# Two orders at the start of a dense block: the third group's first products ahead of the first second product, and the finished rows' norm two calls later

## The chip, the cores and the metric

The kernel runs on one core of a Trainium2 chip. The metric is device time in microseconds (us) of one execution, the median of several runs. The engines are TensorE (PE; its weight loads are PEld), VectorE (DVE), ScalarE (ACT), GpSimd (POOL) and SyncE (SP), which here only issues transfers (DMAs).

## The reference

Four layers are applied in turn to x, 2048 rows by 576, in 32-bit floats: attention, dense, attention, dense, each on a layer norm of x and added back to x. The attention layer is linear attention with 32 heads of 18, on softmax feature maps. The dense layer has 4608 hidden features:

```python
def _A_ref(x, wqkv, w_phi, wo):
    q, k, v = ...                                  # x @ wqkv, 32 heads of 18
    pq, pk = q @ w_phi, k @ w_phi                  # per head
    phi_q = concat(softmax(pq), softmax(-pq)); phi_k = concat(softmax(pk), softmax(-pk))
    kv = sum_s phi_k v;  z = sum_s phi_k
    o = (phi_q kv) / (phi_q z + 1e-6)
    return o @ wo
def _B_ref(x, w1, b1, w2, b2):
    r = relu(x @ w1 + b1)
    return (r * r) @ w2 + b2
x = x + _A_ref(layernorm(x)); x = x + _B_ref(layernorm(x))
x = x + _A_ref(layernorm(x)); x = x + _B_ref(layernorm(x))
```

## The kernel before

The rows are worked in four blocks of 512. One pair of attention and dense is called a layer here (0 and 1). Before each layer's dense blocks a barrier finishes the sums over all keys. Then come four dense blocks, in the order 3, 2, 0, 1 for layer 0 and 1, 0, 3, 2 for layer 1. Names such as m_0acc leave the layer's number out: m_0 is the dense work of block 0, n_0 the norm of block 0's finished rows, a_0 the attention of block 0.

Products are made of high and low halves: a 32-bit operand is split into a rounded high part (a copy on ACT) and the remainder (a subtraction on DVE, for one piece on POOL), and three of the four partial products are summed.

A dense block (`g_mlp`) takes the hidden features in 36 groups of 128. For one group f:

- `first(f)` loads w1's and w2's pieces by SP (lines 666 and 169 for w1, 668 for w2), copies their high halves on ACT (L673 for w1, L674 for w2) and subtracts the low halves (L676 and L677 on DVE, L678 on POOL). It also takes the PSUM tile for the group's hidden values.
- `hidden(f)` is the first product, 14 matmuls (L688): five with the high weights and high rows, four with the low rows, five with the low weights. Groups 0 and 1 are done in two halves of 256 columns, since the last rows of the block arrive late.
- `square(f)` makes the relu (L695), the high square (L696) and the square again (L697) on ACT and the low half on DVE (L698).
- `second(f)` is the second product into five PSUM accumulators: 12 matmuls by rows (L715) and 3 by features (L706). The high squares are read first, the low ones by the last four L715 and the last L706.

The steady step f is first(f + 1), hidden(f), square(f), second(f - 1). After group 35 comes the tail: the last second product, and the adding of the accumulators to the rows x (L755, L759), which are stored and kept for the next block's use.

All this is written as a generator with a yield behind each step, 36 yields in a block. `weave` draws on a second generator, `g_back`, beside it: at rate 1.0 one call for each step, at rate 1.5 (layer 0, blocks 2 to 4 in order) 54 calls in 36 steps, and what is left is drained behind the tail. In layer 0 `g_back` first norms the rows of the block finished just before (`g_norm`, 5 calls: statistics on DVE, L298 and L299; two steps on POOL, L300 and L301; scaling on DVE, L303 and L304; then transposes on PE, L318 and L328, whose results ACT and DVE write in two halves, L319, L320, L330 and L331). Then it makes that block's values (4 calls) and keys (10 calls) for the next layer. Then, in both layers, it makes the attention of the block that comes next (34 calls): queries (L359, L378), softmax, sums, output projections (L642, L645) and the next block's norm. The last call of that is the norm's last turn.

The text's order is not each engine's order. A planner takes, on each engine, the earliest instruction in the text among those that it expects to be ready, by its own durations; the order is fixed when the program is built, and each engine then waits on semaphores. Tiles are taken from rings: two buffers each for the w1 and w2 pieces raw and split, and for the squared values; two PSUM buffers "w" for projections, transposes and group 1's hidden values; one PSUM buffer "h" for the hidden values of all other groups; five buffers for rows x.

Of the kernel before, what the change touches and what calls it, by code (L numbers as in the profile page):

```python
# [13 lines left out]
P = 128  # L14
# [7 lines left out]
def layers_kernel(  # L22
# [632 lines left out]
    def g_mlp(layer, b, x, after, name, behind=None):  # L655

        xh, xl = x["h"], x["l"]
        acc = [ps_a.tile([P, TB], F32, tag=f"acc{c}", name=f"{name}acc{c}") for c in range(NC)]
        parts = {}
        R = D - P  # L660

        def first(f, behind=None):
            cols = slice(f * P, (f + 1) * P)
# [4 lines left out]
            nc.sync.dma_start(r2, w2[cols])  # L668
# [4 lines left out]
            nc.scalar.activation(h1, r1, AF.Copy)  # L673
            nc.scalar.activation(s2[:, :D], r2, AF.Copy)  # L674
            with tc.issue_after(behind.ins) if behind else nullcontext():
                nc.vector.tensor_sub(l1, r1, h1.bitcast(F32))  # L676
                nc.vector.tensor_sub(s2[:, D : D + R], r2[:, :R], s2[:, :R].bitcast(F32))  # L677
            nc.gpsimd.tensor_sub(s2[:, D + R : 2 * D], r2[:, R:], s2[:, R:D].bitcast(F32))  # L678
            ph = wtile(f"{name}ph{f}") if f == 1 else ps_a.tile([P, TB], F32, tag="h", name=f"{name}ph{f}")
            parts[f] = (h1, l1, s2, ph)  # L680

        def hidden(f, cols):
            h1, l1, s2, ph = parts[f]
            ops = [(h1[:, c], xh[:, c, cols]) for c in range(NC)]
            ops += [(h1[:, c], xl[:, c, cols]) for c in range(KC)]
            ops += [(l1[:, c], xh[:, c, cols]) for c in range(NC)]
            for k, (a, m) in enumerate(ops):
                nc.tensor.matmul(ph[:, cols], a, m, start=(k == 0), stop=(k == len(ops) - 1))  # L688

        def square(f):  # L690
            s2, ph = parts[f][2:]
# [3 lines left out]
            nc.scalar.activation(hr, ph, AF.Relu, bias=b1t[:, f : f + 1])  # L695
            nc.scalar.activation(hh, hr, AF.Square)  # L696
            nc.scalar.activation(hr, hr, AF.Square)  # L697
            dense["last"] = nc.vector.tensor_sub(hl, hr, hh.bitcast(F32))  # L698
            parts[f] = (s2, hh, hl)

        def features(f, ks):
            s2, hh, hl = parts[f]
            hi, lo = s2[:, R:D], s2[:, D + R : 2 * D]
            for k in ks:
                a, m = ((hi, hh), (lo, hh), (hi, hl))[k]
                nc.tensor.matmul(acc[KC], a, m, start=(f == 0 and k == 0), stop=(f == NF - 1 and k == 2))  # L706

        def by_rows(f, ts, ks):
            s2, hh, hl = parts[f]
            hi, lo = s2[:, :R], s2[:, D : D + R]  # L710
            for t in ts:
                rows = slice(t * P, (t + 1) * P)
                for k in ks:
                    a, m = ((hh, hi), (hh, lo), (hl, hi))[k]
                    nc.tensor.matmul(acc[t][:, :R], a[:, rows], m, start=(f == 0 and k == 0),  # L715
                                     stop=(f == NF - 1 and k == 2))

        def second(f):

            for ks in ((0, 1), (2,)):  # L720
                by_rows(f, range(NT), ks)
                features(f, ks)
            del parts[f]

        every = slice(0, TB)
        halves = (slice(0, TB // 2), slice(TB // 2, TB))
# [3 lines left out]
        for f in range(2):  # L730
            hidden(f, halves[1])
            square(f)
        second(0)
        yield
        yield
        first(2)
        for f in range(2, NF):
            if f + 1 < NF:
                first(f + 1)
            hidden(f, every)  # L740
            square(f)
            second(f - 1)
            yield
# [100 lines left out]
    for layer in range(2):  # L844
# [4 lines left out]
        for i, b in enumerate(order):  # L849
# [64 lines left out]
```

## Time and profile before

| | |
|---|---|
| median of 3 runs | 2573.97 us (2573.57 to 2576.54) |
| profiled execution, span | 2573.9 us |
| PE busy | 2529.2 us |
| DVE, ACT, POOL busy | 1455.2, 1235.7, 623.0 us |
| HBM traffic | 246.90 MB read, 30.97 MB written |

The profile is of one execution. Its span reaches from the first to the last instruction, and it agrees with the median; no other time of that execution is listed. A row of the order of time has the start, the busy time, the engine, the line, the operation, what is written from what, the sizes and the count; brackets give the idle time before it and what ended it. Matmuls are pipelined, so a row's busy time overlaps the next row's, and the time from start to start is what a matmul costs in a stream.

### The profile page before, as it was taken

To read this page: it belongs to the slowest core of one execution; us is meant where nothing else is said; L and a number is where in the kernel's file an instruction comes from. 1 tells how busy PE (TensorE), PEld (TensorE's weight loads), DVE (VectorE), ACT (ScalarE), POOL (GpSimd) and SP (SyncE) were. 2 spreads that over 40 slices of the span, in tenths; PEclk is the share of its full clock that TensorE was granted. 3 is DMA by queue.
4 is the path that set the end of the run, shared out by engine and by line. 5 is a ranking of instruction groups with operands and counts; after the bars stand their busy time and mean duration, and the time that the engine had idled before them with its cause. 6 is when DMAs were issued, how large, how long until landed. Compare 5 with 4: busy or idle time off the path is not lost.

```text
span 2573.9 us, 41327 instructions
## 1 busy us (share of the span) xinstructions
PE 2529.2 (98%) x15456; PEld 2231.5 (87%) x15456; DVE 1455.2 (57%) x2254; ACT 1235.7 (48%) x2061; POOL 623.0 (24%) x693
## 2 busy tenths in 40 slices
PE   8999999999999999999999999999999999999999
PEld 7998888888888888888888988888888888888887
DVE  7778844456665467556434778444564458444333
ACT  4344554445554455545544445545555455534444
POOL 3543311113222132223111333121231213121111
PEclk9998999999999999999999999999999999999999
DMA  8212333354333543343334123335433353334332
GB/s 251 75 27 67 104 111 87 110 187 129 91 93 113 171 126 97 87 140 101 108 98 122 43 67 103 111 94 161 130 101 88 101 167 103 87 102 130 98 101 79
DMA packets 298020, 280.61 MB, mean 109 GB/s; under 512 B 28186, under 2 KB 238362, under 8 KB 295770
## 3 DMA queue, kind: packets, MB, share of 16 engines
q1 hardware_dynamic: 296560, 275.26, 36.0%
q8 instruction: 121, 1.98, 0.3%
q10 hardware_dynamic: 1258, 2.70, 0.3%
q14 instruction: 81, 0.66, 0.1%
HBM read 246.90 MB, written 30.97 MB: 108 GB/s over the span
## 4 chain that ended last, share of the span: by engine, by line
PE 55%; DVE 3%; POOL 1%; issue 1%; ACT 1%; DMA 0%; DVEq 0%; POOLq 0%; ACTq 0%; SPq 0%
PE m_1ph L688 8%; PE m_0ph L688 6%; PE m_1acc L715 6%; PE m_0acc L715 5%; PE m_2ph L688 5%; PE m_3ph L688 4%; PE m_3acc L715 3%; PE m_2acc L715 3%; PE m_1acc L706 2%; PE m_0acc L706 1%; PE m_2acc L706 1%; PE m_3acc L706 1%; PE a_2po L642 1%; PE t1opo L642 1%; PE k_0kp L359 1%
## 5 line engine op out<-in xcount | busy, mean ns | idle before, releaser
L715 PE MATMUL m_3acc<-m_3s,m_3hb 128*128 128x448 f32 x864 | 199.7, 366 | 1.0 <-DVE m_3hb L698 1.0
L715 PE MATMUL m_1acc<-m_1s,m_1hb 128*128 128x448 f32 x864 | 199.2, 366 | 1.5 <-DVE m_1hb L698 1.5
L715 PE MATMUL m_0acc<-m_0s,m_0hb 128*128 128x448 f32 x864 | 199.3, 366 | 1.3 <-DVE m_0hb L698 1.3
L715 PE MATMUL m_2acc<-m_2s,m_2hb 128*128 128x448 f32 x864 | 199.2, 366 | 1.3 <-DVE m_2hb L698 1.3
L688 PE MATMUL m_0ph<-a_0nh,m_0h 128*128 128x512 f32 (+1 forms) x760 | 192.7, 383 | 0.5 <-DVE m_0h L676 0.5
L688 PE MATMUL m_2ph<-a_2nh,m_2h 128*128 128x512 f32 (+1 forms) x760 | 191.9, 382 | 0.2 <-DVE m_2h L676 0.2
L715 PEld LDWEIGHTS m_0acc<-m_0s,m_0hb 128*128 128x128 f32 x864 | 161.7, 188 | 23.3 <-DVE m_0hb L698 2.2
L715 PEld LDWEIGHTS m_1acc<-m_1s,m_1hb 128*128 128x128 f32 x864 | 161.8, 188 | 23.0 <-DVE m_1hb L698 2.3
L715 PEld LDWEIGHTS m_2acc<-m_2s,m_2hb 128*128 128x128 f32 x864 | 161.8, 188 | 22.9 <-DVE m_2hb L698 2.2
L715 PEld LDWEIGHTS m_3acc<-m_3s,m_3hb 128*128 128x128 f32 x864 | 161.6, 188 | 22.8 <-DVE m_3hb L698 1.4
L676 DVE TENSOR_TENSOR m_2h<-m_2r,m_2h 128x640 fp32r<-128x640 f32 x72 | 62.9, 873 | 182.5 <-ACT m_2h L673 179.9
L688 PEld LDWEIGHTS m_0ph<-a_0nh,m_0h 128*128 128x128 f32 x760 | 136.5, 188 | 27.2 <-DVE m_0h L676 1.0
L688 PEld LDWEIGHTS m_2ph<-a_2nh,m_2h 128*128 128x128 f32 x760 | 136.8, 188 | 26.8 <-DVE m_2h L676 0.7
L676 DVE TENSOR_TENSOR m_3h<-m_3r,m_3h 128x640 fp32r<-128x640 f32 x72 | 66.4, 923 | 157.4 <-ACT m_3h L673 151.0
L676 DVE TENSOR_TENSOR m_0h<-m_0r,m_0h 128x640 fp32r<-128x640 f32 x72 | 65.6, 911 | 154.6 <-ACT m_0h L673 152.8
L676 DVE TENSOR_TENSOR m_1h<-m_1r,m_1h 128x640 fp32r<-128x640 f32 x72 | 64.9, 902 | 155.4 <-ACT m_1h L673 152.5
L678 POOL TENSOR_TENSOR m_2s<-m_2r,m_2s 128x128 fp32r<-128x128 f32 x72 | 61.2, 850 | 362.1 <-ACT m_2s L674 343.5
L678 POOL TENSOR_TENSOR m_0s<-m_0r,m_0s 128x128 fp32r<-128x128 f32 x72 | 58.8, 817 | 351.8 <-ACT m_0s L674 318.7
L678 POOL TENSOR_TENSOR m_3s<-m_3r,m_3s 128x128 fp32r<-128x128 f32 x72 | 59.2, 822 | 342.6 <-ACT m_3s L674 312.3
L695 ACT ACTIVATE m_3hr<-m_3ph,b1t 128x512 f32<-128x512 f32 x72 | 49.5, 687 | 186.6 <-PE m_3ph L688 181.7
L678 POOL TENSOR_TENSOR m_1s<-m_1r,m_1s 128x128 fp32r<-128x128 f32 x72 | 59.6, 828 | 322.0 <-ACT m_1s L674 312.5
L695 ACT ACTIVATE m_0hr<-m_0ph,b1t 128x512 f32<-128x512 f32 x72 | 49.4, 686 | 175.9 <-PE m_0ph L688 173.3
(1535 smaller groups left out, 6376.4 us busy)
## 6 DMA issues: line engine op xcount, KB each, us to landing
m_3r<-in_B_w SPq DMA_DIRECT2D x72, 288.0 KB
m_2r<-in_B_w SPq DMA_DIRECT2D x72, 288.0 KB
m_0r<-in_B_w SPq DMA_DIRECT2D x72, 288.0 KB
m_1r<-in_B_w SPq DMA_DIRECT2D x72, 288.0 KB
m_3r<-in_B_w SPq DMA_DIRECT2D x72, 256.0 KB
m_2r<-in_B_w SPq DMA_DIRECT2D x72, 256.0 KB
m_0r<-in_B_w SPq DMA_DIRECT2D x72, 256.0 KB
m_1r<-in_B_w SPq DMA_DIRECT2D x72, 256.0 KB
```

The costliest lines, as they stand in the source:

```text
L359: nc.tensor.matmul(pt[:, :HP], a, m, start=(k == 0), stop=(k == len(ops) - 1))
L642: nc.tensor.matmul(pt[:, :HP], a, m[:w, g], start=(g == 0 and k == 0), stop=(g == NG - 1 and k == 2))
L676: nc.vector.tensor_sub(l1, r1, h1.bitcast(F32))
L678: nc.gpsimd.tensor_sub(s2[:, D + R : 2 * D], r2[:, R:], s2[:, R:D].bitcast(F32))
L688: nc.tensor.matmul(ph[:, cols], a, m, start=(k == 0), stop=(k == len(ops) - 1))
L695: nc.scalar.activation(hr, ph, AF.Relu, bias=b1t[:, f : f + 1])
L706: nc.tensor.matmul(acc[KC], a, m, start=(f == 0 and k == 0), stop=(f == NF - 1 and k == 2))
L715: nc.tensor.matmul(acc[t][:, :R], a[:, rows], m, start=(f == 0 and k == 0), stop=(f == NF - 1 and k == 2))
```

## The change

`first` is cut in two: `first_one` (w1's piece, its split and the PSUM tile) and `first_two` (w2's piece and its split); `first` calls both. At the start of a dense block, `first_one(2)` and `hidden(2)` are written behind the squares of groups 0 and 1, ahead of the first two yields; `second(0)`, `first_two(2)`, `square(2)`, `first(3)` and `second(1)` stand behind those yields. The loop then runs from group 3. A block still has 36 yields. In `g_back` two bare yields stand ahead of the norm of the finished rows, so that this norm, and what follows it, comes two calls later in blocks 2 to 4 of layer 0.

```diff
+        def first_one(f, behind=None):
             cols = slice(f * P, (f + 1) * P)
             r1 = sb.tile([P, NC, P], F32, tag="r1", name=f"{name}r1_{f}")
-            r2 = sb.tile([P, D], F32, tag="r2", name=f"{name}r2_{f}")
             nc.sync.dma_start(r1[:, :KC], w1[: KC * P, cols].rearrange("(c p) n -> p c n", p=P))
             load_twice(r1[:, KC], w1, f * P, P)
...
+            nc.scalar.activation(h1, r1, AF.Copy)
+            with tc.issue_after(behind.ins) if behind else nullcontext():
+                nc.vector.tensor_sub(l1, r1, h1.bitcast(F32))
+            ph = wtile(f"{name}ph{f}") if f == 1 else ps_a.tile([P, TB], F32, tag="h", name=f"{name}ph{f}")
+            parts[f] = (h1, l1, ph)
+
+        def first_two(f, behind=None):
+            cols = slice(f * P, (f + 1) * P)
+            r2 = sb.tile([P, D], F32, tag="r2", name=f"{name}r2_{f}")
+            nc.sync.dma_start(r2, w2[cols])
             s2 = sb.tile([P, NC * HP], F32R, tag="s2", name=f"{name}s2_{f}")
-            nc.scalar.activation(h1, r1, AF.Copy)
             nc.scalar.activation(s2[:, :D], r2, AF.Copy)
...
         for f in range(2):
             hidden(f, halves[1])
             square(f)
-        second(0)
+        first_one(2)
+        hidden(2, every)
         yield
         yield
-        first(2)
-        for f in range(2, NF):
+        second(0)
+        first_two(2)
+        square(2)
+        first(3)
+        second(1)
+        yield
+        for f in range(3, NF):
             if f + 1 < NF:
                 first(f + 1)
             hidden(f, every)
...
                     xk = {}
+                    yield
+                    yield
                     yield from g_norm(lambda t: rows[t], xk, f"n{m}")
```

More of the change, by code (lines that the diff above doesn't have):

```diff
@@ L658, in g_mlp @@
         acc = [ps_a.tile([P, TB], F32, tag=f"acc{c}", name=f"{name}acc{c}") for c in range(NC)]
-        parts = {}
+        parts, wide = {}, {}
         R = D - P
         def first(f, behind=None):
+            first_one(f, behind)
+            first_two(f, behind)
+        def first_one(f, behind=None):
             cols = slice(f * P, (f + 1) * P)
             r1 = sb.tile([P, NC, P], F32, tag="r1", name=f"{name}r1_{f}")
-            r2 = sb.tile([P, D], F32, tag="r2", name=f"{name}r2_{f}")
             nc.sync.dma_start(r1[:, :KC], w1[: KC * P, cols].rearrange("(c p) n -> p c n", p=P))
             load_twice(r1[:, KC], w1, f * P, P)
-            nc.sync.dma_start(r2, w2[cols])
             hl1 = sb.tile([P, NC * HP], F32R, tag="h1", name=f"{name}h1_{f}")
@@ L671, in first @@
             l1 = hl1[:, NC * P : 2 * NC * P].rearrange("p (c n) -> p c n", n=P)
+            nc.scalar.activation(h1, r1, AF.Copy)
[7 more added lines that the diff above has]
+            nc.sync.dma_start(r2, w2[cols])
             s2 = sb.tile([P, NC * HP], F32R, tag="s2", name=f"{name}s2_{f}")
-            nc.scalar.activation(h1, r1, AF.Copy)
             nc.scalar.activation(s2[:, :D], r2, AF.Copy)
             with tc.issue_after(behind.ins) if behind else nullcontext():
-                nc.vector.tensor_sub(l1, r1, h1.bitcast(F32))
                 nc.vector.tensor_sub(s2[:, D : D + R], r2[:, :R], s2[:, :R].bitcast(F32))
             nc.gpsimd.tensor_sub(s2[:, D + R : 2 * D], r2[:, R:], s2[:, R:D].bitcast(F32))
-            ph = wtile(f"{name}ph{f}") if f == 1 else ps_a.tile([P, TB], F32, tag="h", name=f"{name}ph{f}")
-            parts[f] = (h1, l1, s2, ph)
+            wide[f] = s2
         def hidden(f, cols):
-            h1, l1, s2, ph = parts[f]
+            h1, l1, ph = parts[f]
             ops = [(h1[:, c], xh[:, c, cols]) for c in range(NC)]
@@ L698, in square @@
             dense["last"] = nc.vector.tensor_sub(hl, hr, hh.bitcast(F32))
-            parts[f] = (s2, hh, hl)
+            parts[f] = (hh, hl)
         def features(f, ks):
-            s2, hh, hl = parts[f]
+            s2, (hh, hl) = wide[f], parts[f]
             hi, lo = s2[:, R:D], s2[:, D + R : 2 * D]
@@ L708, in by_rows @@
         def by_rows(f, ts, ks):
-            s2, hh, hl = parts[f]
+            s2, (hh, hl) = wide[f], parts[f]
             hi, lo = s2[:, :R], s2[:, D : D + R]
@@ L722, in second @@
                 features(f, ks)
-            del parts[f]
+            del parts[f], wide[f]
         every = slice(0, TB)
```

2 lines of the change are left out of this document (1 added, 1 removed).

## The prediction

> **What bounds the kernel now.** I read the page first, then the waits of TensorE (PE), then the order of time at the start of a dense block, then at its end.
>
> ```profile
> span 2573.9 us, 41327 instructions
> PE 2529.2 (98%) x15456; PEld 2231.5 (87%) x15456; DVE 1455.2 (57%) x2254; ACT 1235.7 (48%) x2061; POOL 623.0 (24%) x693
> ```
>
> PE is the bound and nothing else is near it. The change issues the same matmuls in another order, so it can only move PE's idle time, which is 2573.9 - 2529.2 = 44.7 us over everything. A gain is small by nature; a loss has no such limit. PE's waits in the first 20 us of dense blocks 2, 3 and 4 of layer 0, in that order, are the ones that the change can reach (waiting instruction, releaser, us in total, times, longest):
>
> ```profile
> PE n_3p L318 <- DVE n_3n L303: 0.5, 1, 0.5
> PE m_2acc L715 <- DVE m_2hb L698: 0.5, 1, 0.5
> PE a_2np L318 <- DVE a_2nn L303: 0.4, 1, 0.4
> PE n_3p L328 <- DVE n_3l L320: 0.2, 1, 0.2
> ```
> ```profile
> PE n_2p L318 <- DVE n_2n L303: 0.5, 1, 0.5
> PE m_0acc L715 <- DVE m_0hb L698: 0.5, 1, 0.5
> PE n_2p L328 <- DVE n_2l L320: 0.4, 1, 0.4
> ```
> ```profile
> PE n_0p L328 <- DVE n_0l L320: 0.5, 1, 0.5
> PE n_0p L318 <- DVE n_0n L303: 0.5, 1, 0.5
> PE m_1acc L715 <- DVE m_1hb L698: 0.5, 1, 0.5
> ```
>
> The same three in each block: a transpose of the finished rows waits for their scaling (L318 on L303); the second product waits for the low half of the squared values (L715 on L698); a later transpose waits for a PSUM buffer to be emptied (L328 on L320). The order of time shows why, here in the third block (start us, us, engine, line, what, idle before):
>
> ```profile
> 837.38 0.69 ACT L695 ACTIVATE m_0hr<-m_0ph,b1t 128x512 f32<-128x512 f32 x1 [4.13 <-PE m_0ph L688]
> 837.97 0.73 ACT L673 ACTIVATE m_0h<-m_0r 128x640 fp32r<-128x640 f32 x1
> 838.25 0.75 PE L688 MATMUL m_0ph<-a_0nh,m_0h 128*128 128x256 f32 x5
> 838.87 0.55 DVE L303 TENSOR_SCALAR n_2n<-m_2x,n_2m,n_2d 128x512 f32<-128x512 f32 x1 [0.68 <-POOL n_2d L301]
> 839.48 0.55 PE L318 MATMUL n_2p<-ident,n_2n 128*128 128x128 f32 x3 [0.48 <-DVE n_2n L303]
> 839.68 0.63 ACT L697 ACTIVATE m_0hr<-m_0hr 128x512 f32<-128x512 f32 x1
> 839.78 1.89 PE L715 MATMUL m_0acc<-m_0s,m_0hb 128*128 128x448 f32 x8
> 841.51 0.63 PE L706 MATMUL m_0acc<-m_0hb,m_0s 128*128 128x512 f32 x2
> 841.86 0.67 DVE L698 TENSOR_TENSOR m_0hb<-m_0hr,m_0hb 128x512 fp32r<-128x512 f32 x1
> 842.58 0.77 DVE L676 TENSOR_TENSOR m_0h<-m_0r,m_0h 128x640 fp32r<-128x640 f32 x1
> 842.59 1.09 PE L715 MATMUL m_0acc<-m_0s,m_0hb 128*128 128x448 f32 x4 [0.45 <-DVE m_0hb L698]
> ```
>
> Call T the end of the first products of groups 0 and 1: five matmuls from 838.25 at 0.12 each, about 838.85. Nothing is ready for PE then, and three transposes that the text has behind the second product were planned into the hole; their rows are late and PE starts again at 839.48. The low half of group 0 could be made at 840.31 (839.68 + 0.63) and is made at 841.86, behind norm work on VectorE. A stall costs more than its idle time: two L706 matmuls from 841.51 at 0.23 spacing hand over at 841.97, and the next starts at 842.59, so 0.62 is lost where 0.45 is listed.
>
> **The change, part by part.** A hidden group and a second product, from the steady state:
>
> ```profile
> 783.79 1.32 PE L688 MATMUL m_2ph<-a_2nh,m_2h 128*128 128x512 f32 x5
> 785.88 1.30 PE L688 MATMUL m_2ph<-a_2nh,m_2h 128*128 128x512 f32 x5
> 787.01 1.79 PE L715 MATMUL m_2acc<-m_2s,m_2hb 128*128 128x448 f32 x8
> 790.13 0.30 PE L642 MATMUL a_0po<-a_0o0h,a_0oh 126*128 126x288 f32 x1
> ```
>
> Hidden(2) is 3.2 us of PE work (783.79 to 787.01), a second product 3.1 (787.01 to 790.13); the low weights are first read 2.1 us into a hidden group.
>
> *Hidden(2) at T.* It needs its high weights, copied by ACT at 837.97 to 838.70, before T by 0.15. The copy keeps its place: in the text it is behind both squares as before, and it runs where it does because its buffer comes free with group 0's products. So PE goes on at T, and the first stall, 838.85 to 839.48, goes: 0.6 us in each of three blocks. With so little margin a first weight load may be late; bounds 0 and 0.5 (the L318 wait), I take 0.05 in each of eight blocks, as 0.15 is still a margin: 0.4.
>
> *The low weights of group 2.* They are due at T + 2.1 = 840.95 and were made at 842.58 to 843.35. They were ready to be made from 838.70; they came late since the norm's VectorE work stood ahead of them in the text. Now they stand ahead of it. Behind the one scaling already begun (838.87 + 0.55) they end by 840.2. No cost, bounds 0 and 2.4 (843.35 - 840.95); the upper one is a rival below.
>
> *The second product of group 0* starts at T + 3.2 = 842.05 instead of 839.78. Its low half is read 2.4 us later (842.59 - 0.45 of idle, less 839.78), at 844.4, and was ready at 842.53 even with the norm's work ahead of it. The second stall goes: 0.62 in three blocks. Group 1's second product follows at once; all its inputs are older.
>
> *What the move makes wait.* The squares of group 2 share two buffers with group 0, so ACT's first square of group 2 waits for the second product of group 0 to end (T + 6.3), and so does its second weight. Behind it on ACT stand the low square and those weight copies; then VectorE and GpSimd subtract: 0.63 + 0.63 + 0.67 makes T + 8.3, and the second product of group 2 comes at T + 6.3 + 3.1 + 3.2 = T + 12.6. Hidden. In blocks of layer 1 where query projections (calls 1 and 2) now stand ahead of the second product, everything slides together. [...]
>
> *DMAs.* The first weight's three transfers go out ahead of calls 1 and 2 and the second weight's one behind the second product; both were issued far ahead of use already, and T + 12.6 leaves the latter over 6 us after its buffers are free. Nothing.
>
> *The norm two calls later.* Only layer 0 blocks 2 to 4 have it. Its transposes come with the slots behind steps 3 to 5, where PE has steady work. The third stall (0.2, 0.4, 0.5 listed, 0.4 to 0.6 lost, 1.6 in all) comes of three requests for two PSUM buffers in one slot; in the new timing turn 1, its rest and turn 2 again share a slot, but VectorE is less crowded there. Bounds 0 and 1.6; I take 1.2.
>
> *The last slot.* At rate 1.5, 36 steps give 54 calls. The work beside blocks 2 and 3 has 5 + 4 + 10 + 34 = 53, now 55: the last turn of the next block's norm falls behind the block's tail. The end of block 2 now:
>
> ```profile
> 825.71 0.60 PE L318 MATMUL a_0np<-ident,a_0nn 128*128 128x128 f32 x4
> 827.35 1.66 DVE L273 TENSOR_TENSOR w_2v1l<-w_2v1r,w_2v1h 128x1440 fp32r<-128x1440 f32 x1
> 827.89 2.61 PE L715 MATMUL m_2acc<-m_2s,m_2hb 128*128 128x448 f32 x12
> 831.09 0.55 DVE L303 TENSOR_SCALAR a_0nn<-a_0x,a_0nm,a_0nd 128x512 f32<-128x512 f32 x1 [0.51 <-POOL a_0nd L301]
> 831.69 0.66 PE L318 MATMUL a_0np<-ident,a_0nn 128*128 128x128 f32 x4 [0.36 <-DVE a_0nn L303]
> 833.73 0.43 DVE L331 TENSOR_TENSOR a_0nh<-a_0np,a_0nh 64x256 fp32r<-64x256 f32 x1
> ```
>
> From the end of the last output projection (825.7) to the last norm piece (834.16) are 8.5 us, a weight split of 1.66 on VectorE among them. PE has beside it, with the 1.2 us of group 34's second product now ahead of the projections: the tail (0.7 + 2.4), the transposes (0.4 + 0.5 + 0.5), and group 0 and 1's first halves (2 x 1.7), 7.9, and the 0.36 stall that is there already. About 0.2 us short, less than one stall; I take it as nothing, bounds -0.4 (that stall goes) and the rival's.
>
> *The other five blocks* have no rows to norm. In two of layer 1 a short hole before the second product goes: two L359 matmuls at 0.13 hand over at 1796.61, the next starts at 1796.78; with the pipeline's restart I take 0.25 each, 0.5 in all.
>
> ```profile
> 1796.35 0.43 PE L359 MATMUL a_3qp<-a_3q0h,a_3uh 128*128 128x288 f32 x2
> 1796.78 1.89 PE L715 MATMUL m_0acc<-m_0s,m_0hb 128*128 128x448 f32 x8
> ```
>
> **The sum.** 3 x (0.63 + 0.62) = 3.8, + 1.2, + 0.5, - 0.4 = 5.1; 2573.9 - 5.1 = 2568.8 us. The span of the profiled execution and the median of the runs (2573.97) agree within 0.1 us. About 0.2% (5.1 us) is what a measurement of this kernel can tell from no change, so the forecast stands on that edge.
>
> **Rivals.** *The stalls only move.* PE's order is a plan, and the three waits are plan against chip; norm work in new slots may meet new ones of 0.4 to 0.6. For: other waits of that kind stay in the same blocks. Against: the waits that go are named and get 2 us of cover. Three stalls of 0.62 back in each block would leave 2573.9 + 0.4 - 0.5 + 0.6 = 2574.4; two back, 2572.5, which I take.
>
> *The low weights are late.* If VectorE's order keeps them behind the norm as at 842.58, hidden(2) stops at its tenth matmul for 2.4 us in three blocks: 7.2 lost against 5.1 gained, 2576.0. It decides from 1.7 us a block. Against: they stand ahead in the text now.
>
> *The last turn is uncovered*, the way to slower. If PE has used up the tail as filler while projections wait for PSUM, only the two half groups and their transposes (3.9) cover 8.5: 4.6 us at the ends of blocks 2 and 3. The clock then matters:
>
> ```profile
> 215.00:220.00 5.00, 2.88 (x22) 2.33 (x21) 3.44 (x8) 2.81 (x8) 2.93 (x4) 0.99 0.01 2
> 220.00:225.00 5.00, 2.96 (x12) 2.26 (x12) 5.00 (x12) 1.22 (x4) 3.05 (x2) 0.50 0.00 0
> 225.00:230.00 5.00, 4.87 (x23) 4.25 (x23) 4.61 (x12) 2.08 (x6) 1.16 (x1) 0.50 0.00 0
> 835.00:840.00 5.00, 4.52 (x38) 4.32 (x37) 4.32 (x15) 2.62 (x5) 0.91 (x3) 1.00 0.93 311
> ```
>
> (Window; its length; busy PE, PEld, DVE, ACT, POOL; granted clock; DMA.) Where PE idled 2 us in 5 the granted clock fell to 0.50 for 10 us, and 7.8 us of matmuls ran at half speed: 3.9 lost. A 0.5 us hole kept 1.00. So 2 x (4.6 + 3.9) - 5.1 = +11.9, 2585.8; without the clock 2578.0. It decides from 2.6 us a block. [...]
>
> **How the numbers follow.** The forecast 0.60, of it 0.44 faster by over 0.2% and 0.16 within, as its terms can be a little less (own range 2566.0 to 2571.5); stalls that only move 0.13, within; low weights late 0.09, 0.05 within and 0.04 slower; uncovered last turn 0.14, slower; other slips of the shifted slots 0.04, slower. Faster 0.44, same 0.34, slower 0.22. The range 2565.5 (all bounds in favour, 5.1 + 0.4 + 0.4 + 0.8 and some slack) to 2577.5 takes in the late low weights and leaves out the uncovered turn.
>
> **What would show it.** Right: at T hidden(2) starts with no idle time; L715 on L698 and L318 on L303 are gone from PE's waits at the starts of blocks 2 to 4; two second products run back to back. Wrong: PE waits on L676 nine matmuls into hidden(2); waits on L303, L320 or L331 at the starts of blocks 3 and 4 with a granted clock below 1; ACT stuck at L696 with L319 or L378 behind it.

## The result: slower by 0.24%, and the profile after

The changed kernel took 2579.96 us in the median (2578.66 to 2582.88), the kernel before 2574.6 us beside it. The ratio is 1.0024 with a 95% interval of 1.0016 to 1.0032. The forecast was 2568.8 us with a range up to 2577.5; its sign was wrong, and the time lies outside the range.

From the page of the changed kernel, the span and the busy times:

```profile
span 2580.3 us, 41338 instructions
PE 2530.3 (98%) x15456; PEld 2234.6 (87%) x15456; DVE 1458.5 (57%) x2254; ACT 1237.6 (48%) x2061; POOL 625.9 (24%) x693
```

The matmuls are the same in number, and the span is 6.4 us longer. In the changed kernel the numbers of lines are higher: L697 is `hidden`, L706 and L707 the squares, L715 and L724 the second product, L687 and L688 the two subtractions for w2's low part. In kernels with further edits these numbers are up to three higher again.

**The starts of the blocks did get better.** In order of time, the start of the second block of layer 0 in the changed kernel (start us, us, engine, line, what; idle time would stand in brackets):

```profile
522.80 1.93 PE L697 MATMUL m_2ph<-a_2nh,m_2h 128*128 128x256 f32 x10
523.88 0.82 DVE L676 TENSOR_TENSOR m_2h<-m_2r,m_2h 128x640 fp32r<-128x640 f32 x1
525.48 1.29 PE L697 MATMUL m_2ph<-a_2nh,m_2h 128*128 128x512 f32 x5
526.61 1.78 PE L724 MATMUL m_2acc<-m_2s,m_2hb 128*128 128x448 f32 x8
528.70 0.97 PE L724 MATMUL m_2acc<-m_2s,m_2hb 128*128 128x448 f32 x4
529.75 1.78 PE L724 MATMUL m_2acc<-m_2s,m_2hb 128*128 128x448 f32 x8
```

Group 2's first product follows with no idle time, its low weights (L676 at 523.88) are in time for the products at 525.48, and the second products of groups 0 and 1 run back to back. The waits of PE in the first 20 us of the second block and then of the third in the changed kernel (the fourth has the third's, with the same sizes):

```profile
PE a_2np L318 <- DVE a_2nn L303: 0.4, 1, 0.4
```
```profile
PE a_0np L318 <- DVE a_0nn L303: 0.5, 1, 0.5
PE m_0ph L697 <- ACT a_0nh L319: 0.3, 1, 0.3
PE m_0ph L697 <- DVE m_0h L676: 0.2, 1, 0.2
PE m_0ph L697 <- DVE a_0nl L320: 0.2, 1, 0.2
```

The three waits of before that the prediction named are gone. Of the four rows of the third block the first stood there before the change too, nearly as long:

```profile
PE a_0np L318 <- DVE a_0nn L303: 0.4, 1, 0.4
```

The other three, 0.7 us in all, are new in the third and fourth blocks. Two of them, and the first row, belong to the last turn of the block's own norm; the one on L676 is for the low weights of group 2. How much work PE got done in those 20 us is read from windows (window, length, busy PE, PEld, DVE, ACT, POOL, granted clock, DMA share, GB/s). Kernel before, starts of the second, third and fourth blocks:

```profile
515.06:535.06 20.00, 18.52 (x117) 16.12 (x116) 16.56 (x41) 10.18 (x19) 7.88 (x13) 1.00 0.74 244
830.34:850.34 20.00, 18.26 (x116) 15.90 (x115) 16.68 (x40) 9.95 (x18) 7.23 (x13) 1.00 0.74 248
1145.86:1165.86 20.00, 18.25 (x116) 15.89 (x115) 16.70 (x40) 9.93 (x18) 6.92 (x13) 1.00 0.74 242
```

The changed kernel, the same 20 us from each block's first matmul:

```profile
514.89:534.89 20.00, 19.64 (x122) 17.81 (x121) 16.46 (x40) 10.60 (x18) 7.06 (x14) 1.00 0.66 215
835.81:855.81 20.00, 18.81 (x114) 16.48 (x113) 16.53 (x39) 10.15 (x18) 8.21 (x13) 1.00 0.73 234
1156.18:1176.18 20.00, 18.79 (x114) 16.47 (x113) 16.49 (x39) 10.13 (x18) 8.76 (x13) 1.00 0.72 234
```

PE is busy 1.12, 0.55 and 0.54 us longer there: a gain of 2.2 us in all.

**The loss is in the middle of the second and third blocks.** From the first `hidden` matmul of one block to that of the next, the second block took 315.3 us before and 320.9 after, the third 315.5 and 320.4: +5.6 and +4.9. The way from the fourth block's start to that of layer 1's second dense block became 3.3 us shorter, and the rest of the program 0.8. PE's longest waits over the whole second block, before (515.06 to 830.34) and after (514.89 to 835.81):

```profile
PE m_2acc L715 <- DVE m_2hb L698: 1.3, 2, 0.8
```
```profile
PE m_2acc L724 <- DVE m_2hb L707: 3.5, 2, 2.7
PE k_3kp L359 <- DVE kv L447: 1.8, 1, 1.8
```

The wait of 1.8 us in the changed kernel, in order of time. It is a key projection waiting for a PSUM buffer that VectorE empties (L447 adds the product of keys and values to its sum):

```profile
620.67 2.40 POOL L411 TENSOR_TENSOR k_3K2e<-k_3K2e,k_3K2r 128x1152 f32<-128x1152 f32 x1 [3.93 <-DVE k_3K2r L404]
620.99 2.57 DVE L687 TENSOR_TENSOR m_2s<-m_2r,m_2s 128x448 fp32r<-128x448 f32 x1
623.59 0.46 DVE L447 TENSOR_TENSOR kv<-kv_1k,kv 128x288 f32<-128x288 f32 x1
624.10 0.94 PE L359 MATMUL k_3kp<-w_3k1h,n_3h 128*128 128x288 f32 x5 [1.80 <-DVE kv L447]
```

VectorE has hardly a pause there, as the window of these 5 us says (start and end, length, busy PE, PEld, DVE, ACT, POOL, granted clock, DMA share, GB/s):

```profile
620.00:625.00 5.00, 3.20 (x49) 2.92 (x37) 4.97 (x6) 2.61 (x4) 3.31 (x4) 1.00 0.25 69
```

The wait of 2.7 us, the changed kernel again:

```profile
705.13 0.75 DVE L556 TENSOR_REDUCE a_0u<-a_0m 128x32 f32<-128x576 f32 x1 [1.33 <-POOL a_0m L555]
705.80 1.34 DVE L403 TENSOR_REDUCE a_0Q3r<-a_0Q3e 128x64 f32<-128x1152 f32 x1
707.06 0.74 DVE L556 TENSOR_REDUCE a_0u<-a_0m 128x32 f32<-128x576 f32 x1
708.89 0.68 DVE L707 TENSOR_TENSOR m_2hb<-m_2hr,m_2hb 128x512 fp32r<-128x512 f32 x1
709.62 1.08 PE L724 MATMUL m_2acc<-m_2s,m_2hb 128*128 128x448 f32 x4 [2.68 <-DVE m_2hb L707]
```

The sum of the last softmax (L403, piece Q3) now stands on VectorE between two sums of the feature maps (L556 begins at 705.13 and 707.06), and the low half of the squares (L707), which PE needs, comes behind them at 708.89, though its input was ready at 704.90 (L706 on ACT, 704.29 + 0.61). VectorE is not busy all this time: it first waits 1.33 us for GpSimd's share of the feature map (L555, from 703.14), which began behind GpSimd's subtraction for the same softmax (L400, 701.56 to 703.18). Before, the last softmax had ended when the feature sums began, as the groups by line of the kernel before show (durations in ns, then the first and last start):

```profile
L403 DVE TENSOR_REDUCE a_0Q3r<-a_0Q3e x1: 1354/1354/1354, 689.4 to 689.4; 128x64 f32<-128x1152 f32 x1
L556 DVE TENSOR_REDUCE a_0u<-a_0m x5: 734/739/740, 694.0 to 711.2; 128x32 f32<-128x576 f32 x5
```

Why these meet now follows from the rate. At 1.5 calls a step, steps draw one call and two calls in turn, so every second step has a pair. Two more calls ahead of all others are not a multiple of the three calls that two steps draw, so the pairs fall elsewhere. There are three possible pairings: with the calls counted from 1 as before the change, the pairs are (2, 3), (5, 6) and so on before, and (3, 4), (6, 7) and so on after. Calls 26 and 27 (the softmax of Q2 and of Q3) shared a step before; now calls 24 and 25 and calls 27 and 28 do, and the latter pair is the last softmax with the first half of the first feature sum. The keys' calls were re-paired in the same way.

In the second block each of the two long waits is followed by a lower granted clock, in the third block the same waits aren't (windows of the changed kernel, columns as above; 945.90 is where the third block's key projection goes on after its 1.7 us):

```profile
624.10:631.00 6.90, 6.90 (x29) 5.97 (x30) 5.16 (x5) 1.70 (x2) 0.83 (x1) 0.75 0.78 264
709.60:717.00 7.40, 7.38 (x26) 6.16 (x27) 7.40 (x10) 1.91 (x4) 4.37 (x3) 0.77 0.41 128
945.90:953.00 7.10, 7.04 (x38) 6.31 (x39) 5.55 (x7) 3.39 (x5) 1.03 (x3) 1.00 0.79 277
```

The rows of the first stretch show two speeds: the five matmuls of L697 from 626.41 took 2.13 us (to 628.54), the five of the same shape from 629.72 took 1.16 (to 630.88). Taking the clock as either whole or half, an estimate from the windows: 0.75 over 6.90 us means 2 x 0.25 x 6.90 = 3.4 us at half speed, and 0.77 over 7.40 us the same 3.4 us. So by this estimate a wait costs another 1.7 us in these two places, where the clock drops. The whole blocks show both parts. Windows over the second and third blocks, before and then after:

```profile
515.06:830.34 315.28, 312.45 (x1900) 273.13 (x1899) 186.63 (x277) 155.35 (x251) 76.68 (x85) 1.00 0.40 120
830.34:1145.86 315.52, 312.37 (x1900) 273.18 (x1899) 187.28 (x278) 155.07 (x250) 76.51 (x85) 1.00 0.40 120
```
```profile
514.89:835.81 320.92, 315.18 (x1903) 276.36 (x1902) 187.43 (x278) 155.74 (x251) 76.89 (x84) 0.99 0.38 117
835.81:1156.18 320.37, 312.65 (x1900) 273.33 (x1898) 189.25 (x278) 155.53 (x250) 78.55 (x84) 1.00 0.39 118
```

In the second block PE is idle 320.92 - 315.18 = 5.7 us where it was 2.8, and its busy time is 2.7 us longer; the slower clock shows in that (two drops of the estimated 1.7 us would make 3.4). In the third it is idle 7.7 us where it was 3.2, at a granted clock of 1.00.

### The profile page after: what moved, and what is told of

Same layout as the page of the kernel before. It is cut to its first block, busy times and chain, and to the rows that moved or that the text cites. A ratio compares the mean times of both kernels' runs of the same rounds, so it can differ in the third digit from the quotient of the medians.

```text
span 2580.3 us, 41338 instructions
## 1 busy us (share of the span) xinstructions
PE 2530.3 (98%) x15456; PEld 2234.6 (87%) x15456; DVE 1458.5 (57%) x2254; ACT 1237.6 (48%) x2061; POOL 625.9 (24%) x693
## 4 chain that ended last, share of the span: by engine, by line
PE 54%; DVE 4%; POOL 1%; issue 1%; ACT 0%; DVEq 0%; POOLq 0%; ACTq 0%
PE m_1ph L697 8%; PE m_1acc L724 6%; PE m_0ph L697 6%; PE m_2ph L697 4%; PE m_3ph L697 4%; PE m_0acc L724 4%; PE m_3acc L724 3%; PE m_2acc L724 3%; PE m_1acc L715 2%; PE m_0acc L715 1%; PE m_2acc L715 1%; PE m_3acc L715 1%; PE a_2po L642 1%; PE a_1po L642 1%; PE t1opo L642 1%
## 5 line engine op out<-in xcount | busy, mean ns | idle before, releaser
L724 PE MATMUL m_0acc<-m_0s,m_0hb 128*128 128x448 f32 x864 | 199.5, 366 | 4.8 <-DVE m_0hb L707 4.8
L724 PE MATMUL m_2acc<-m_2s,m_2hb 128*128 128x448 f32 x864 | 199.4, 366 | 3.5 <-DVE m_2hb L707 3.5
L724 PE MATMUL m_3acc<-m_3s,m_3hb 128*128 128x448 f32 x864 | 199.4, 366 | 1.0 <-DVE m_3hb L707 1.0
L724 PE MATMUL m_1acc<-m_1s,m_1hb 128*128 128x448 f32 x864 | 198.9, 365 | 1.0 <-DVE m_1hb L707 1.0
L697 PE MATMUL m_0ph<-a_0nh,m_0h 128*128 128x512 f32 (+1 forms) x760 | 192.1, 383 | 0.7 <-ACT a_0nh L319 0.3
L697 PE MATMUL m_2ph<-a_2nh,m_2h 128*128 128x512 f32 (+1 forms) x760 | 192.5, 385 | 0.0
L724 PEld LDWEIGHTS m_0acc<-m_0s,m_0hb 128*128 128x128 f32 x864 | 161.6, 188 | 27.0 <-DVE m_0hb L707 6.2
L724 PEld LDWEIGHTS m_2acc<-m_2s,m_2hb 128*128 128x128 f32 x864 | 161.8, 188 | 24.9 <-DVE m_2hb L707 4.4
L724 PEld LDWEIGHTS m_1acc<-m_1s,m_1hb 128*128 128x128 f32 x864 | 162.0, 188 | 22.1 <-DVE m_1hb L707 1.4
L724 PEld LDWEIGHTS m_3acc<-m_3s,m_3hb 128*128 128x128 f32 x864 | 161.7, 188 | 22.3 <-DVE m_3hb L707 1.4
L676 DVE TENSOR_TENSOR m_2h<-m_2r,m_2h 128x640 fp32r<-128x640 f32 x72 | 61.1, 849 | 188.6 <-ACT m_2h L674 185.5
L697 PEld LDWEIGHTS m_2ph<-a_2nh,m_2h 128*128 128x128 f32 x760 | 138.0, 190 | 26.6
L697 PEld LDWEIGHTS m_0ph<-a_0nh,m_0h 128*128 128x128 f32 x760 | 136.5, 188 | 27.9 <-DVE m_0h L676 0.7
L676 DVE TENSOR_TENSOR m_1h<-m_1r,m_1h 128x640 fp32r<-128x640 f32 x72 | 64.6, 899 | 154.0 <-ACT m_1h L674 147.8
L676 DVE TENSOR_TENSOR m_0h<-m_0r,m_0h 128x640 fp32r<-128x640 f32 x72 | 64.5, 897 | 152.4 <-ACT m_0h L674 148.6
L676 DVE TENSOR_TENSOR m_3h<-m_3r,m_3h 128x640 fp32r<-128x640 f32 x72 | 65.6, 912 | 149.9 <-ACT m_3h L674 149.9
L688 POOL TENSOR_TENSOR m_2s<-m_2r,m_2s 128x128 fp32r<-128x128 f32 x72 | 60.4, 839 | 357.6 <-ACT m_2s L685 351.7
L688 POOL TENSOR_TENSOR m_0s<-m_0r,m_0s 128x128 fp32r<-128x128 f32 x72 | 58.4, 812 | 339.6 <-ACT m_0s L685 299.1
L688 POOL TENSOR_TENSOR m_3s<-m_3r,m_3s 128x128 fp32r<-128x128 f32 x72 | 58.5, 813 | 331.7 <-ACT m_3s L685 289.9
L688 POOL TENSOR_TENSOR m_1s<-m_1r,m_1s 128x128 fp32r<-128x128 f32 x72 | 60.0, 833 | 308.3 <-ACT m_1s L685 300.7
L704 ACT ACTIVATE m_1hr<-m_1ph,b1t 128x512 f32<-128x512 f32 x72 | 49.5, 688 | 169.7 <-PE m_1ph L697 168.3
```

## The experiments

Ratios are to the kernel before on the same chip, with 95% intervals. One theory says that the pairing of calls makes the loss, another that the order inside the dense block does, a third that the last turn of the norm comes too late. The expectations call them the phase theory, the order theory, and the late-work or delay theory.

**The order alone.** The changed kernel without its two bare yields:

```diff
                     xk = {}
-                    yield
-                    yield
                     yield from g_norm(lambda t: rows[t], xk, f"n{m}")
```

> The change without the two calls: hidden(2) ahead of the first second product, the norm of the finished rows where it was before. Phase theory (the two extra calls change which calls beside the dense steps share a step, three calls to two steps, and so pile VectorE work up in the middle of the second and third block of layer 0): the stalls of 1.8 to 2.8 us in the middle of those blocks are gone, and what is left is the gain at the starts: 3 to 5 us faster than before. Order theory (the new order of the first groups is what costs): 4 us or more slower than before. Late-work theory (everything beside the block comes later and its last call falls behind the tail): as the phase theory, about 2 to 4 us faster.

Measured: 2570.57 us, 0.9989 (0.9980 to 0.9998). The second and third blocks took 314.6 and 314.9 us, a little less than before. One wait has grown: the transposes of the finished rows, which waited 0.2 to 0.5 us for a PSUM buffer before (L328 on L320), now wait 1.2 in each of the three blocks, so a part of the gain is lost again. In the second block:

```profile
PE n_3p L328 <- DVE n_3l L320: 1.2, 1, 1.2
```

The same kernel beside another experiment, its neighbour (the last one below):

> The new order alone once more, beside the run with one yield less on the same chip: 3 to 4 us faster than before, and within 2 us of its neighbour. If the norm's delay is worth something by itself, its neighbour is 1 to 2 us faster.

Measured: 2571.0 us, 0.9992 (0.9983 to 1.0001). The order of the dense block is a small gain, about 0.1%, and is not where the loss comes from. The neighbour measured 2568.39 us, 2.6 less and so a little outside the 2 us of the expectation: with the old pairing in the middle and no call behind the tail, the later norm seems to be a gain of its own.

**The two yields alone.** The kernel before with the same two yields:

```diff
                     xk = {}
+                    yield
+                    yield
                     yield from g_norm(lambda t: rows[t], xk, f"n{m}")
```

> The two calls alone, in the kernel before; the first groups stay in their old order. Phase theory: the mid-block stalls of the changed kernel are all there and the gain of the order is missing at the starts but for the waits that come from norm work: 7 to 11 us slower than before. Order theory: within 2 us of before. Late-work theory: 5 to 10 us slower, too.

Measured: 2586.66 us, 1.0056 (1.0042 to 1.0070), with blocks of 320.8 and 321.7 us. That is more than the 7 to 11 us expected (12.9 by the medians). The yields bring the loss. The parts don't add up: alone they come to -0.0011 + 0.0056 = +0.0045, together to +0.0024. One reason is a wait at the start of the third block that the yields make in the old order:

```profile
PE m_0acc L715 <- DVE m_0hb L698: 1.7, 1, 1.7
```

The fourth block has the same with 1.8 us. In the changed kernel group 2's first product stands in that place, and neither wait is there. So the new order does hide the late second product, as it says.

**The pairing alone.** The kernel before with nothing but the counter of `weave` started at 1.0 at the higher rate. The first step draws one call more, and the pairs are those of the changed kernel, (3, 4), (6, 7) and so on:

```diff
-        due = 0.0
+        due = 1.0 if rate > 1.0 else 0.0
```

> The kernel before, with nothing but the count of due calls begun at 1.0 where the rate is 1.5: each call comes at the same step as before or one step earlier, nothing comes later, no order is changed in the dense block, and the calls that share a step are those of the changed kernel (the last softmax with the first half of the first feature sum, and so on). Phase theory: the same stalls in the middle of the second and third block, 6 to 12 us slower than before. Late-work theory and order theory: no slower than before, within 2 us.

Measured: 2585.07 us, 1.0046 (1.0034 to 1.0059), blocks of 320.8 and 320.6 us. Its waits in the second block:

```profile
PE m_2acc L715 <- DVE m_2hb L698: 3.9, 3, 2.7
PE k_3kp L359 <- DVE kv L447: 1.8, 1, 1.8
```

The dense block is in its old order, no call is added, and every call comes in its old step or one step earlier; still the waits of 2.7 and 1.8 us are there, to the tenth. So lateness doesn't make them; they go with the pairing.

**The old pairing, with the change.** The changed kernel with the counter started at 0.5; behind the two bare calls the pairs are again those of before, (2, 3), (5, 6) and so on:

```diff
-        due = 0.0
+        due = 0.5 if rate > 1.0 else 0.0
```

> The whole change, with the count of due calls begun at 0.5 where the rate is 1.5. Calls 1 and 2 (the bare ones) then share step 1 and the norm begins alone in step 2: all that is drawn beside the block comes exactly one step later than in the kernel before, with the same calls sharing a step, and the last call still falls behind the tail. Phase theory: the mid-block stalls are no more than before (about 1 us in all of a block), so 1 to 4 us faster than before. Late-work theory: still 4 to 6 us slower than before, as the last call is as late as in the changed kernel. Order theory: 4 us or more slower.

Measured: 2573.89 us, 1.0000 (0.9991 to 1.0009); blocks of 314.4 and 316.0 us. Waits in the second block:

```profile
PE m_2acc L724 <- DVE m_2hb L707: 0.9, 1, 0.9
PE n_3p L328 <- DVE n_3l L320: 0.8, 1, 0.8
```

The two long waits are gone and the loss with them: 0.0024, or 6.2 us, give or take some 3 us, as each ratio has its interval. The gain of the order alone, and the 1 to 4 us expected, don't come, though: in the first 10 us of the third and the fourth blocks together PE is idle 3.9 us, against 0.7 with the order alone. There the last turn of the norm runs behind the block's tail.

**The third pairing.** The kernel of the order alone with the counter at 0.5, which makes the pairs (1, 2), (4, 5) and so on:

> The new order alone, with the count of due calls begun at 0.5 at rate 1.5: the third of the three ways in which calls can share steps (calls 1 and 2, 4 and 5, and so on; the last softmax with nothing, the first feature sum's second half with nothing); nothing is later than before. Phase theory alone says only that mid-block stalls differ; if they come from softmax and feature sum in one step, there is no stall over 1.5 us and the time is within 4 us of the run with the order alone, 2567 to 2574.

Measured: 2573.68 us, 0.9996 (0.9987 to 1.0005), blocks of 315.0 and 317.1 us. The second block has no single wait over 1.2 us; the third has one of 1.9 us at the key projection, over the 1.5 that the expectation allowed. So the three pairings differ, and that of the changed kernel is the worst. Why that one wait is in the third block and not in the second is open.

**Three yields.** With a third yield the pairs after it fall where they fell before the change:

```diff
                     yield
                     yield
+                    yield
                     yield from g_norm(lambda t: rows[t], xk, f"n{m}")
```

> The whole change with three bare calls instead of two. Three calls are two whole steps, so the calls that share a step are those of the kernel before, and all comes two steps later; two calls instead of one fall behind the tail. Phase theory: the mid-block stalls of 1.8 and 2.8 us are absent, and the kernel is 3 to 7 us faster than the changed kernel although it delays more; the ends of the second and third block may cost 2 us more than in the run with two calls drawn early. Delay theory (the later, the worse): slower than the changed kernel.

Measured: 2583.13 us, 1.0031 (1.0019 to 1.0043). The expectation was missed, but the second block took 313.1 us and has no wait over 0.8: three calls later, the pairing is the old one and the waits are gone. The loss is at the next block's start, where now two calls are behind the tail. PE's waits there (829 to 845), and the window behind them:

```profile
PE a_0np L318 <- DVE a_0x L645: 3.1, 1, 3.1
PE a_0np L318 <- DVE a_0nn L303: 2.4, 1, 2.4
```
```profile
834.00:839.00 5.00, 2.22 (x11) 1.58 (x11) 4.14 (x14) 1.27 (x3) 2.33 (x4) 0.65 0.79 246
```

With the lower clock that is, by an estimate, about 7 us at each of two starts: 5.5 us of waits at the first (3.1 + 2.4) and 5.3 at the second (2.9 + 2.4), and some 2 us for matmuls at a clock of 0.66 (839 to 844) and of 0.50 (1158 to 1163). The second of two late calls costs far more than the first. Little of the old block's work is left to cover it; and at the third block's start VectorE's addition L645, which PE waits for, was itself held for 1.14 us by the transfer of the rows a_0x.

**The late last turn alone.** The order alone, with two bare yields ahead of the next block's norm only. All earlier pairs stay as they were; the last turn comes behind the tail:

```diff
+        if layer == 0 and name[0] == "a" and b < NB - 2:
+            yield
+            yield
         yield from g_norm(x_after, dst, f"{name}n", keep)
```

> The new order, with the two bare calls moved from ahead of the finished rows' norm to ahead of the next block's norm: the middle of the blocks is as with the order alone, and only the last five calls come two calls later, the last of them behind the tail, as in the changed kernel. It measures the late last turn by itself: 1.5 to 2 us at each start of the third and fourth block, so 3 to 4 us slower than the order alone (about 2574), with no stall over 1.1 us in the middle. If the late turn costs nothing, 2570 to 2571.

Measured: 2576.3 us, 1.0008 (0.9999 to 1.0016), so 0.0019 or 4.9 us above the order alone (give or take some 3 us), more than expected. The waits at the third block's start are those of the changed kernel, and one more (832 to 855), and behind it the clock drops to 0.66 over 5 us; the fourth block's start has the same wait:

```profile
PE n_2p L328 <- DVE n_2l L320: 1.9, 1, 1.9
```
```profile
849.00:854.00 5.00, 4.85 (x17) 4.34 (x18) 3.92 (x8) 2.18 (x4) 0.90 (x1) 0.66 0.83 261
```

**One pair taken apart.** The changed kernel with one bare yield between the last softmax and the feature sums:

```diff
+        if layer == 0 and b < NB - 2:
+            yield
         yield from held(g_phi(layer, er, ph, name, True))
```

> The whole change and one more bare call between the four softmax calls and the feature sums, in the second and third block of layer 0. Up to the softmax all calls share steps as in the changed kernel, from there on as in the kernel before. Phase theory by pile-up: the stall of 2.8 us at the second product goes, with its half-speed matmuls, and the stall of 1.8 us at the keys' projection stays; 3 to 6 us faster than the changed kernel in the middle of the blocks, less up to 2 us for a second call behind the tail: 2574 to 2578. If the stalls hang on something else than softmax and feature sum in one step, both stay and it is no faster than the changed kernel.

Measured: 2586.69 us, 1.0045 (1.0032 to 1.0058), against the expectation. The waits in the second block:

```profile
PE k_3kp L359 <- DVE kv L447: 1.8, 1, 1.8
PE m_2acc L724 <- DVE m_2hb L707: 1.5, 1, 1.5
```

The 2.7 became 1.5, so that pair was a part of it and not all; the key projection, earlier in the block, is untouched. The added call put a second one behind the tail, and the third block's start has waits of 3.1 and 2.0 us, much as in the run with three yields. What makes the remaining 1.5 is open.

**VectorE's subtraction beside GpSimd's multiplication.** The subtraction L687 took 2.57 us beside GpSimd's multiplication L411, where 0.63 is usual (the median in the changed kernel). Here that multiplication goes to VectorE for the keys of the two blocks:

```diff
-        nc.gpsimd.tensor_mul(e3, e3, r2.unsqueeze(2).to_broadcast([P, 2 * H, DH]))
+        eng = nc.vector if name[:4] in ("k1_3", "k1_2") else nc.gpsimd
+        eng.tensor_mul(e3, e3, r2.unsqueeze(2).to_broadcast([P, 2 * H, DH]))
```

> The whole change, with the scaling of the softmaxed keys (L411, 2.4 us on GpSimd) done by VectorE in the blocks 3 and 2. In the changed kernel VectorE's subtraction L687, 0.6 us by itself, took 2.57 us beside it, and the sum of keys and values that empties PE's PSUM buffer stood behind it. If GpSimd's multiplication holds VectorE up, the stalls of 1.8 us at the keys' projection go, with their half-speed matmuls, no L687 takes over 1.0 us there, and the stall of 2.7 us at the second product stays: 2 to 6 us faster than the changed kernel. If VectorE is only short of time there, the stall stays or grows, as the multiplication adds some 1.2 us of work to it: 0 to 4 us slower.

Measured: 2578.73 us, 1.0022 (1.0013 to 1.0031), as the changed kernel. In the second block:

```profile
620.42 0.88 DVE L688 TENSOR_TENSOR m_2s<-m_2r,m_2s 128x448 fp32r<-128x448 f32 x1
```
```profile
PE m_2acc L725 <- DVE m_2hb L708: 3.7, 2, 2.7
PE k_3kp L359 <- DVE kv L448: 1.4, 1, 1.4
```

The slow subtraction is gone, and the wait went only from 1.8 to 1.4 there; VectorE has the multiplication itself now (1.34 us), so the run can't tell the slowing from the work that was added. But the kernel before had such a slowing too: beside the multiplication of the same piece K2 its low half of the squares (L698, at 616.24) took 2.65 us, and PE did not wait. So the slowing by itself isn't the cause; there is too much for VectorE in that stretch.

**The last turn back in its slot, by two dropped yields.** The changed kernel with the counter at 0.5, and with two of the bare yields in the output part (`g_out`) dropped for those blocks:

```diff
+        short = layer == 0 and name[0] == "a" and b < NB - 2
         pair = pieces() if behind else None
-        yield
+        if not short:
+            yield
...
-        yield
+        if not short:
+            yield
         pair = pair or pieces()
```

> The whole change with the count of due calls begun at 0.5 at rate 1.5, and two yields of the attention's output stage left out in the second and third block of layer 0, so that 53 calls are left and none falls behind the tail. The norm then comes one step later, the calls up to the output stage share steps as in the kernel before, and the next block's norm is no later than before. If the two costs of the change are the calls that share steps and the late last turn, and nothing else, both are gone: as fast as the order alone or 1 to 2 us better, 3 to 5 us faster than before (2569 to 2571 beside 2574). If the delay of the norm has a cost of its own, 2573 or more.

Measured: 2581.73 us, 1.0030 (1.0018 to 1.0041), against the expectation. The blocks' starts are as good as with the order alone, but a new wait stands in the second block:

```profile
PE a_0pt L595 <- DVE a_0Q3e L565: 4.3, 1, 4.3
```

The first of the dropped yields had kept the scaling of the queries (L565) a slot ahead of the transposes that read it (L595). A bare yield is not always empty time.

**By one dropped yield.** The changed kernel with the counter at 0.5 and only the second of them dropped; that makes 54 calls for 54 slots:

```diff
...
-        yield
+        if not (layer == 0 and name[0] == "a" and b < NB - 2):
+            yield
         pair = pair or pieces()
```

> As the run with the early end, but only the one yield ahead of the output weights' split is left out; the yield between the last feature sum and the first transposes of the output stage is back, so the transposes are a call behind what they read. 54 calls for 54 slots: none behind the tail. If the 4.3 to 4.5 us stalls of the early end came from that missing yield and the changed kernel's cost from shared steps and the late turn alone, no stall over 1.1 us is left in the middle of the second and third block, their starts lose what they lose with the order alone or less, and the time is 2568 to 2571 beside 2574 for before. If the transposes still wait, or the norm's delay has a cost of its own, 2573 or more.

Measured: 2568.39 us, 0.9981 (0.9973 to 0.9990): faster than both kernels, as expected. The blocks take 313.7 and 313.8 us, and the longest waits in each are 0.9 and 0.8 us, those of the old pairing with the change.

Against the same kernel with 55 calls (1.0000) that is 0.0019 less, as much as the late last turn cost when it was added to the order alone. Each of the two differences is uncertain by some 3 us, and both edits also change which of the last few calls share a step, so the 4.9 us is the price of the late end as a whole.

## Why the prediction was wrong

- **What bounds the kernel**, and that a loss has no such limit as a gain: right. The order of the work on PE changed nothing in the work itself.
- **Hidden(2) at T, and the second product of group 0**: right in mechanism. The waits named are gone from all three starts, and the second products run back to back. The size was 3.8 us with 1.2 for the third stall; PE got 2.2 us more done in the three windows, since new waits took part of it back in two of them. In the second block alone, where no late turn disturbs, 1.12 stands against 1.25 + 0.4. By the two runs with the order alone, all but the norm's term was worth 0.0008 to 0.0011 of the time, 2.1 to 2.8 us, where the sum had 3.9.
- **The low weights of group 2**: right that they don't hold PE for long. The wait on L676 came in the third and fourth blocks, at 0.2 us and not 2.4.
- **The other five blocks**: right. Four of them became 0.1 to 0.3 us shorter each, the first of layer 1 stayed as it was.
- **The norm two calls later** is the step that failed. It looked at where the norm's own transposes would land and took a gain of 1.2. That part did come: the wait of L328 on L320 is gone in the changed kernel. The prediction treated the delay as a delay of the norm, but `g_back` is one chain: the two yields shift all of the 53 calls that follow, and at three calls in two steps a shift by two changes which calls share a step. That re-paired the keys and the softmaxes, 100 to 200 us behind the block's start, where VectorE was busy 4.97 of 5 us at one of the waits, and at the other worked and waited for GpSimd in turn. The runs put its price at 0.0024, 6.2 us (the change with its own pairing against the change with the old one), and the pairing alone, with no other edit, at 0.46%. The prediction had this only as "other slips of the shifted slots", with a chance of 0.04 and no working.
- **The last slot** was taken as nothing: "About 0.2 us short", that is 0.2 us of cover missing. In the changed kernel the late turn has 1.0 us of listed waits at each of two starts (0.5, 0.3, 0.2), of which 0.4 stood there before; by itself, added to the order alone, it costs 4.9 us. The rival of the uncovered last turn named the place, and was nearer in size (4.6 us an end) to the run with three yields than to the changed kernel. The 6.2 us of the pairing and these 4.9 are 11.1 together, and the changed kernel came out 11.2 above the forecast; with some 3 us of doubt on each, that they fit so well is in part luck.
- **The clock.** The prediction's rows had a drop to 0.50 where PE idled 2 us in 5, and in the rival of the uncovered last turn it put 3.9 us on each drop. In the changed kernel a single wait of 1.8 us was followed by a drop in one place (0.75 over 6.90 us), and the third block's 2.6 us was not (1.00 over 7.10 us). A drop there cost 1.7 us, estimated from the two windows of the second block, and not 3.9.

The kernel with one yield less took 4.9 us less than the kernel before (0.0019 of 2573.4), where the forecast's sum was 5.1. It has the new order, the later norm, the old pairing as far as the output part, and no call behind the tail. So the forecast's total fits this kernel rather than the changed one, but that the two agree so closely is luck: the interval is 2.6 to 7 us, the order gave less than its 3.9 (2.1 to 2.8), and the later norm, so far as two neighbours on one chip show it, more than its 1.2 (2.6).

Two things stay open. The way from the fourth block to layer 1's second dense block became 3.3 us shorter, of which the start window explains 0.5 and the waits at the barrier's transposes 0.7. The clock gives some 1.7 more, an estimate (5 x 0.08 + 5 x 0.26): in the barrier of the kernel before it was 0.92 and 0.74 in two windows of 5 us (1465 to 1475), in the changed kernel 1.00 in the same place (1472 to 1482). Why it dropped in the one and not in the other isn't shown, and it is one execution of each. And the pairing in the keys' part was not taken apart call by call, so which of VectorE's instructions there is the one too many isn't shown.

## What to carry to other kernels

Where two streams are interleaved at a rate that is not whole, an added or removed call is not local: list which calls share a step before and after, over the whole length, and look at the fullest engine at each new pair. Count the calls against the slots as well; one call too many ran behind the tail and cost about as much as the whole change was to gain. And an edit that loses may hold a gain: with the pairing and the count put right, the same order was faster by 0.19%.

## What the runs showed of the hardware that was not expected

- The clock after a wait isn't told by the wait's length alone. In the changed kernel it fell after waits of 1.8 and 2.7 us in the second block (0.75 over 6.90 us, 0.77 over 7.40 us) and stayed at 1.00 after the 1.7, 2.6 and 1.5 us of the third. After the waits of 1.7 and 1.8 us at the starts with the two yields alone it stayed at 1.00 too; after the 1.9 us of the late last turn alone it fell (0.66 over 5 us). Over the changed kernel and three of the experiments, six of the eight waits of 2.6 to 2.7 us were followed by a lower clock (0.77 or 0.78 over some 7 us); most of those of 1.4 to 1.9 us were not (1.00 over some 7 us). So equal waits end differently here, and what decides it is not shown.
- The subtraction of 128x448 on VectorE took 2.57 us beside GpSimd's multiplication of 128x1152 (2.40 us), and as long in six such places of the kernel before (2568 to 2576 ns), and 0.88 us with that multiplication moved to VectorE. In the place at 620.99 the subtraction began 0.32 us behind the multiplication and ended 0.49 us after it. Why the two run so is not shown.
